# Bucketed attention with two expert layers: q and k read head columns first instead of being transposed on the chip

## The chip, the cores and the metric

The kernel runs on one core of one Trainium2 chip. The metric is the device time of one execution in microseconds (us), the median of several runs. The engines are TensorE (PE in the profile, PEld for its weight loads), VectorE (DVE), ScalarE (ACT), GpSimd (POOL) and SyncE (SP, which only issues transfers). Each works through its own instructions in the order in which they were written. The words q, k, v, s, p are the tiles of the attention, as below.

## The reference, cut to what matters

```python
def _attn_ref(q, k, v, proj):                    # q, k, v: (2, 8, 768, 64); proj: (64, 6)
    scale = 1.0 / np.sqrt(D)
    q_bits = (np.einsum('bhsd,dk->bhsk', q, proj) > 0).astype(np.int64)
    k_bits = (np.einsum('bhsd,dk->bhsk', k, proj) > 0).astype(np.int64)
    q_bucket = np.sum(q_bits * powers, axis=-1)
    k_bucket = np.sum(k_bits * powers, axis=-1)
    mask = q_bucket[:, :, :, None] == k_bucket[:, :, None, :]
    scores = scale * np.matmul(q, k.transpose(0, 1, 3, 2))
    scores = np.where(mask, scores, -1000000000.0)
    attn = np.exp(scores - np.max(scores, axis=-1, keepdims=True))
    attn = attn / (np.sum(attn, axis=-1, keepdims=True) + 1e-09)
    return np.matmul(attn, v)
...
x = attn_out.transpose(0, 2, 1, 3).reshape(B * S, H * D)
x = _moe_ref(x, ...)     # 8 experts, each token goes to one: relu(x @ w1[e]) @ w2[e], with two gates
return _moe2_ref(x, ...) # elu(x @ w_in) @ w_out
```

Sixteen heads of 768 tokens and 64 columns are attended; a query only sees the keys whose six projection signs equal its own. Then come a layer of eight experts and a dense layer.

## The kernel before

**Precision.** Matrix products run on operands split in two: hi is the value rounded by ScalarE to the fast format (fp32r), lo is the rest, computed by VectorE as value minus hi.

**Operands of a head.** The scores of a head come from four tiles of 128 rows by 768 columns, opnd[st, "qa"/"qb"/"ka"/"kb"], in four sets st = head % 4. Rows 0 to 63 of qa hold q hi, rows 64 to 127 q lo; ka holds k hi twice; rows 0 to 63 of qb hold q hi, of kb k lo. Rows 64 and up of qb and kb hold the signs of the projection (the bucket), scaled so that a pair of tokens in unlike buckets gets a large negative score. The first and the third 32 rows of that part are constants (constant_rows) or come from a tile z of signs.

**Tiles.** A tile n is 128 queries of one head; a head has 6, a pair of heads 12, the kernel 96 (8 pairs, counted 0 to 7). One turn of the loop at L951 does the following for several tiles at once, in this order: stage_M(n-1), the row maximum nm of the scores on VectorE (L367) and from it the scale sc and bias bi on GpSimd (L368, L369); what the list early holds; stage_T(n-3), six transpositions of the probabilities p on TensorE (L396) with hi on ScalarE (L398) and lo on VectorE (L399), in two halves; stage_S(n), four matmuls of scores into s (L349); stage_V(n-6), four matmuls with v (L413); stage_E(n-1), the exponential p on ScalarE (L376); now and then stage_O, the result o (L442), and stage_R, matmuls with the identity and the gate weights (L489). s has two buffers, so the scores of tile n wait for the exponential of tile n-2.

**Preparing a pair.** Beside the tiles of pair pr the operands of pair pr+1 are made, in six steps prep(pr+1, i), i = 0 to 5. Steps 0 to 3 are prep_T for q and k, in two halves of 384 tokens each: three TensorE transpositions of raw tokens (tokens on partitions, the columns of both heads side by side) into a PSUM tile prep (L212), hi from it on ScalarE (L217), lo on VectorE (L221 for q, L223 for k). When both halves of q or k stand, restack issues six transfers on SP that copy the rows of each head to their places in the operands (L300). Steps 4 and 5 are prep_Z: four matmuls with the projection (L278), and the sign compare on VectorE (L287); after the second, restack issues six small transfers of z. In pairs 1 to 6 the transposing steps are written after tiles 1, 2, 4 and 5 of the pair and finished in the next turn, so they lie in the six tiles that begin with the second; the steps of prep_Z come after tiles 7 and 8. In pair 0 the six steps come after tiles 3 to 8.

**Raw loads.** load_pair reads q and k of a pair as 128 partitions by 6 tokens by 64 columns, in runs of 64 values (L134), two transfers for q and two for k; v comes in one (L128).

**The opening.** Before the loop (L621 to L659) pair 0 is transposed the same way. Head 0's operands are copied into place by ScalarE and GpSimd (L635 to L640) and by three transfers (place, L656), head 1's by restack. The signs of the first keys come from first_Zk (two halves, three matmuls each) and those of the first queries from prep_Zm (six matmuls a half), both on hi and lo; first_Ze writes them straight into kb and qb of head 0 (L251). keep_warm runs matmuls on ones until the first data are there.

## Time and profile before

| what | us |
|---|---|
| median of three runs (lowest to highest) | 712.93 (712.04 to 713.87) |
| the profiled execution's own time | 713.77 |
| its span, from the first instruction to the last | 712.0 |
| attention tiles, first scores to last scores | 9.1 to 243.9 |
| TensorE busy in the span | 698.5 (98%) |
| VectorE / ScalarE busy in the span | 553.7 / 428.4 |

The profile is one execution. A group of rows gives, for one line and engine, a count and durations; the timeline gives single instructions with their start in us from the span's start and, in brackets, the idle time of the engine before one and what ended it. The stretches give, for a piece of the span, each engine's busy time and its number of instructions, then TensorE's granted clock (1.00 is 2.4 GHz), the share of the transfer engines and GB/s. Matmuls overlap, so TensorE's pace is read from the distance between starts.

### The profile page before, as it was taken

The page shows a single profiled execution, that of the slowest core. Times are in us where ns is not written, and L with a number is a line of the kernel's source. Part 1 is how long each engine was busy: PE and PEld are TensorE (multiplying, and loading weights), DVE is VectorE, ACT ScalarE, POOL GpSimd, SP SyncE. Part 2 cuts the span into 40 slices and gives each one's busy share as a digit, 9 for nine tenths or more (in the row PEclk, how much of TensorE's full clock was granted, in tenths as well). Part 3 has the DMA queues.
Part 4 walks back from the last instruction along what each step waited for, and adds up shares of the span by engine and source line. Part 5 has one row for each costly group of instructions (what it writes and reads, how often), then busy time and mean ns, then how long its engine had stood idle before and what let it go on. Part 6 is the DMA issues. An engine that isn't in the chain of part 4 may idle for free.

```text
span 712.0 us, 12226 instructions
## 1 busy us (share of the span) xinstructions
PE 698.5 (98%) x4211; PEld 626.8 (88%) x4212; DVE 553.7 (78%) x1046; ACT 428.4 (60%) x855; POOL 211.1 (30%) x508
## 2 busy tenths in 40 slices
PE   8999999999999999999999999999999999999996
PEld 6899999999998988999999998788888888888884
DVE  6989898899998997788888887877788547934433
ACT  6988888888888865666666665445443224422221
POOL 7665445455456661221065311000000000002012
PEclk9999999999999999999999999999999999999998
DMA  8857758686691239788878986322222000001011
GB/s 188 198 136 178 186 129 210 163 189 164 144 233 57 84 116 299 239 261 242 261 209 247 256 217 144 104 88 75 89 87 92 2 0 1 0 1 60 0 60 62
DMA packets 108596, 97.39 MB, mean 137 GB/s; under 512 B 33480, under 2 KB 94728, under 8 KB 108528
## 3 DMA queue, kind: packets, MB, share of 16 engines
q1 hardware_dynamic: 106064, 90.15, 47.3%
q0 software_dynamic: 2304, 6.40, 2.4%
q8 instruction: 35, 0.57, 0.3%
q14 instruction: 33, 0.27, 0.1%
q10 hardware_dynamic: 160, 0.00, 0.0%
HBM read 64.15 MB, written 10.72 MB: 105 GB/s over the span
## 4 chain that ended last, share of the span: by engine, by line
issue 32%; PE 23%; DMA 6%; POOL 1%; ACT 0%; SPq 0%; POOLq 0%; ACTq 0%
PE hps L1135 11%; PE yps L1148 7%; DMA out_dram<-part,tidt 5%; PE yps L1150 3%; DMA xs<-xs_d 1%; PE xTp L1117 1%; DMA tidt<-tid_d 1%; PE yps L1147 0%; POOL xs L857 0%; POOL out_dram L1293 0%; ACT sum L1153 0%; POOL spacer L612 0%; SPq L743 0%; POOLq L1293 0%; ACTq L1153 0%
## 5 line engine op out<-in xcount | busy, mean ns | idle before, releaser
L399 DVE TENSOR_TENSOR ptlo<-t,pthi 128x384 fp32r<-128x384 f32 x192 | 99.9, 548 | 14.7 <-ACT pthi L398 13.1
L376 ACT ACTIVATE p<-s,bi,sc 128x768 f32<-128x768 f32 x96 | 95.9, 999 | 17.5 <-POOL bi L369 15.7
L832 DVE TENSOR_TENSOR wl<-wraw,wh 128x1024 fp32r<-128x1024 f32 (+1 forms) x65 | 77.4, 1194 | 23.7 <-ACT wh L828 21.4
L367 DVE TENSOR_REDUCE nm<-s 128x1 f32<-128x768 f32 x96 | 90.9, 947 | 0.3 <-PE s L349 0.3
L398 ACT ACTIVATE pthi<-t 128x384 fp32r<-128x384 f32 x192 | 84.8, 497 | 10.2 <-PE t L396 8.9
L1293 POOL DMA_INDIRECT out_dram<-part,tidt x12 | 11.5, 960 | 263.5 <-DVE part L1290 262.2
L1255 ACT ACTIVATE ee<-gps 128x512 f32<-128x512 f32 x48 | 28.7, 597 | 98.0 <-PE gps L1245 98.0
L1148 PE MATMUL yps<-h,wh 128*128 128x448 f32 x256 | 84.4, 380 | 0.0
L396 PE MATMUL t<-ident,p 128*128 128x128 f32 x576 | 79.5, 273 | 0.0
L1245 PE MATMUL gps<-x2h,vl 128*128 128x512 f32 x192 | 75.9, 395 | 0.0
L1275 PE MATMUL a<-vh,gh 128*128 128x512 f32 x192 | 75.6, 394 | 0.0
L1275 PE MATMUL a<-vh,gl 128*128 128x512 f32 x192 | 75.4, 393 | 0.0
L1245 PE MATMUL gps<-x2h,vh 128*128 128x512 f32 x192 | 75.3, 392 | 0.0
L1245 PE MATMUL gps<-x2l,vh 128*128 128x512 f32 x192 | 75.2, 392 | 0.0
L1275 PE MATMUL a<-vl,gh 128*128 128x512 f32 x192 | 74.9, 390 | 0.0
L349 PE MATMUL s<-ka,qa 128*128 128x384 f32 x192 | 73.4, 383 | 1.2 <-DMA qa<-qlo 0.4
L1258 ACT ACTIVATE gh<-ee 128x512 fp32r<-128x512 f32 x48 | 30.4, 633 | 69.2 <-DVE ee L1257 69.2
L1256 DVE TENSOR_SCALAR ee<-ee 128x512 f32<-128x512 f32 x48 | 20.4, 426 | 66.3 <-ACT ee L1255 66.2
L396 PEld LDWEIGHTS t<-ident,p 128*128 128x128 f32 x576 | 67.4, 140 | 3.9 <-DVE ptlo L399 0.5
L828 ACT ACTIVATE wh<-wraw 128x1024 fp32r<-128x1024 f32 x63 | 66.2, 1052 | 2.7 <-DMA wraw<-in_moe_w_dram 2.7
L413 PE MATMUL o<-pthi,vst 128*128 128x384 f32 x192 | 66.9, 349 | 0.3
L349 PE MATMUL s<-kb,qb 102*128 102x384 f32 x192 | 65.3, 341 | 0.4 <-DMA kb<-z 0.4
(224 smaller groups left out, 1768.8 us busy)
## 6 DMA issues: line engine op xcount, KB each, us to landing
wraw<-in_moe_w_dram SPq DMA_DIRECT2D x64, 512.0 KB
w<-in_moe_w_in_dram SPq DMA_DIRECT2D x16, 512.0 KB
w<-in_moe_w_out_dram SPq DMA_DIRECT2D x16, 512.0 KB
ka<-khi SPq DMA_DIRECT2D x30, 192.0 KB
xs_d<-zt SPq DMA_DIRECT2D x8, 528.0 KB
xs<-xs_d SPq DMA_DIRECT2D x8, 528.0 KB
raw_v<-in_v_dram SPq DMA_DIRECT2D x8, 384.0 KB
kb<-klo SPq DMA_DIRECT2D x15, 192.0 KB
```

Source lines behind the costliest of these rows:

```text
L349: nc.tensor.matmul(ps[:, j, 0:HC], opnd[st, "q" + x][0:n1, cb], opnd[st, "k" + x][0:n1, j * HC:(j + 1) * HC], start=(x == "a"), stop=(x == ...
L367: nc.vector.tensor_reduce(nm, sps[n][:, :, 0:HC], AX.XY, ALU.max, negate=True)
L376: nc.scalar.activation(p.rearrange("p (a b) -> p a b", a=2), sps.pop(n)[:, :, 0:HC], AF.Exp, bias=bi, scale=sc, accum_out=sums[hd][:, c:c ...
L396: nc.tensor.transpose(ps[:, a, :], p[:, kt * 128:(kt + 1) * 128], ident)
L398: nc.scalar.activation(ho, ps, AF.Copy)
L399: nc.vector.tensor_tensor(lo[:, HALF * g:HALF * (g + 1), i * 128:(i + 1) * 128], ps, ho, ALU.subtract)
L413: nc.tensor.matmul(ops[m], vst[hd][:, kt, :], t[:, kt, :], start=(kt == 0 and x == 0), stop=(kt == NC - 1 and x == 1))
L832: fs = [lambda c=slice(j, j + h): eng.tensor_tensor(lo[:, c], r[:, c], hi[:, c], ALU.subtract) for j in range(0, PW, h)]
L1135: nc.tensor.matmul(ps, w[:, dc, fs], x[:, dc], start=(i == 0), stop=(i == len(terms) - 1))
L1148: nc.tensor.matmul(ps, wh[:, f], h[:, :, f], start=(f == 0), stop=last)
L1245: nc.tensor.matmul(ps, w[:, dc], x[:, dc, th * TC:(th + 1) * TC], start=(dc == 0 and i == 0), stop=(dc == KD - 1 and i == 2),)
L1275: nc.tensor.matmul(ps, x[:, cs], w, start=(fb in first_fb and i == 0), stop=(fb in last_fb and i == 2))
```

## The change

numpy now lays q and k out head by head with the 64 columns on partitions and the 768 tokens along them, each head twice: the array of one batch and pair has 256 rows, (head 0, head 0, head 1, head 1). The middle 128 rows are one head over the other, which is what prep_T had from its transpositions, so load_pair reads these in one transfer, in runs of 768 values, and prep_T takes hi and lo straight from the raw tile in SBUF. The six steps of pair 0 come one tile later (i = s - 4).

Heads 0 and 1 no longer go through prep_T and restack. load_twice reads each of them doubled (128 rows), and hi and lo are written in place by key_high, key_low, query_high, query_again and query_low: head 0 before the loop, the second half of its queries in turns 0 and 1, and head 1 partly before the loop (key_high) and partly after tiles 1 to 4 (the at(...) lines). The signs of head 0 come from the raw values with unsplit fp32 weights, one matmul a half (hash_of); those of head 1 from its finished operands (second_Z, four matmuls a half), compared by second_Ze and sent on by three transfers.

```diff
@@ load_pair, load_twice @@
-                t = ap2.tile([128, NC, 2 * D], F32, tag="raw_" + nm, name="raw_" + nm, bufs=2 if nm == "q" else 1)
...
-                        nc.sync.dma_start(
-                            t[:, c0:c0 + step, hh * D:(hh + 1) * D],
-                            src[b, h0 + hh].rearrange("(p c) d -> p c d", c=NC)[:, c0:c0 + step],
-                        )
+                t = ap2.tile([128, S], F32, tag="raw_" + nm, name="raw_" + nm, bufs=2 if nm == "q" else 1)
+                nc.sync.dma_start(t, src[b, h0 // 2, D:3 * D])
...
+    def load_twice(hd, nm, js, eng=nc.sync):
+        src = (q if nm == "q" else k)[0, 0, 2 * D * hd:2 * D * (hd + 1)]
...
+        cs = slice(js[0] * HC, (js[-1] + 1) * HC)
+        eng.dma_start(twice[hd, nm][:, cs], src[:, cs])
+
+    load_twice(0, "k", (0,))
+    load_twice(0, "q", (0,), nc.scalar)
+    load_twice(0, "k", (1,))
@@ prep_T @@
-        r = raw[pr, nm]
-        ps = prep_psum("prep")
-        for c in range(HALF):
-            cc = HALF * j + c
-            nc.tensor.transpose(ps[:, c * 128:(c + 1) * 128], r[:, cc, :], ident)
+        ps = raw[pr, nm][:, sl]
@@ heads 0 and 1 @@
+    def key_high(hd, j):
+        nc.scalar.activation(opnd[hd, "ka"][:, half(j)], twice[hd, "k"][:, half(j)], AF.Copy)
+
+    def key_low(hd, j, eng=nc.vector):
+        o, x, h = (t[0:64, half(j)] for t in (opnd[hd, "kb"], twice[hd, "k"], opnd[hd, "ka"]))
+        eng.tensor_tensor(o, x, h, ALU.subtract)
+
+    def query_high(hd, j):
+        nc.scalar.activation(opnd[hd, "qa"][:, half(j)], twice[hd, "q"][:, half(j)], AF.Copy, scale=SCALE)
...
+    def query_low(hd, j, c0=0, c1=HC):
+        cs = slice(j * HC + c0, j * HC + c1)
+        o, x = (t[64:128, cs] for t in (opnd[hd, "qa"], twice[hd, "q"]))
+        nc.vector.scalar_tensor_tensor(o, x, SCALE, o, ALU.mult, ALU.subtract)
+
+    def hash_of(ps, nm, j, i):
+        nc.tensor.matmul(ps, bdf[0:64, i], twice[0, nm][0:64, half(j)], start=True, stop=True)
...
+    def second_Z(j):
+        zps[1, j] = prep_psum("zps")
+        for i, (w, t, n) in enumerate(((0, "qa", 128), (2, "qa", 64), (1, "ka", 128), (1, "kb", 64))):
+            nc.tensor.matmul(
+                zps[1, j], bdr[0:n, w], opnd[1, t][0:n, half(j)], start=(i == 0), stop=(i == 3)
+            )
...
+        nc.vector.tensor_scalar(zt[0][0:64, half(j)], zps.pop((1, j))[0:64], 0.0, None, ALU.is_gt)
+        if j == 1:
+            restack(0, "z", (1,))
@@ the opening @@
+    load_twice(0, "q", (1,))
+    load_twice(1, "k", range(2))
+    load_twice(1, "q", range(2))
+    load_pair(0, "v")
+    load_pair(1)
+    keep_warm(8)
+    for j in range(2):
+        hash_of(zk[:, j, 0:HC], "k", j, 0)
+        key_high(0, j)
+    first_Zq(0)
+    query_high(0, 0)
+    query_again(0, 0, nc.scalar)
+    key_low(0, 0)
+    key_low(0, 1, nc.gpsimd)
...
+    query_high(0, 1)
+    for j in range(2):
+        key_high(1, j)
+    query_again(0, 1, nc.gpsimd)
@@ turns 1 to 4 @@
+    at(1, first_Zq, 1)
+    for i in range(2):
+        at(1 + i, query_high, 1, i)
+        at(2 + i, query_again, 1, i, nc.gpsimd)
+        at(2 + i, key_low, 1, i)
+        at(3 + i, query_low, 1, i)
+        at(3 + i, second_Z, i)
+        at(3 + i, lambda i=i: early.append(lambda: second_Ze(i)))
...
-            i = s - 3 if pr == 0 else s // 3 * 2 + s % 3 - 1 if s % 3 else -1
+            i = s - 4 if pr == 0 else s // 3 * 2 + s % 3 - 1 if s % 3 else -1
```

How this moves the instructions is shown at three places. A number behind a tile's name is only its buffer.

TensorE in the opening, up to the first scores of tile 0, before (zps takes the signs of the first queries, prep is a transposition, s the scores):

```order
L238 MATMUL zps<-qhi,bdh 128x384
L238 MATMUL zps<-qlo,bdh 128x384
L238 MATMUL zps<-qhi,bdl 128x384
L238 MATMUL zps<-khi,bdh 128x384
L238 MATMUL zps<-klo,bdh 128x384
L238 MATMUL zps<-khi,bdl 128x384
L212 MATMUL prep<-ident,raw_q 128x128 x3
L349 MATMUL s<-ka_130,qa_128 128x384 x2
```

The same place after, from the last warming matmul:

```order
L656 MATMUL warm<-ones_b 128x384
L263 MATMUL zk<-k_112,bdf 128x384 x2
L263 MATMUL zps<-q_114,bdf 128x384
L381 MATMUL s<-ka_124,qa_122 128x384 x2
L381 MATMUL s<-kb_125,qb_123 128x384 x2
```

Twelve transpositions and twelve sign matmuls ahead of the first scores (nine transpositions were ahead of the rows shown) have become three fp32 matmuls on the raw tiles.

VectorE in turns 1 to 4, from the maximum of tile 0 (nm), before; z is the sign compare of both heads:

```order
L367 TENSOR_REDUCE nm<-s 128x1
L221 SCALAR_TENSOR_TENSOR qlo<-prep,qhi 128x384
L367 TENSOR_REDUCE nm<-s 128x1
L251 TENSOR_SCALAR qb_129<-zps,thr,amp 38x384
L258 TENSOR_SCALAR z<-zps 128x384
L367 TENSOR_REDUCE nm<-s 128x1
L399 TENSOR_TENSOR ptlo<-t,pthi 128x3x128 x2
L258 TENSOR_SCALAR z<-zps 128x384
```

The same place after, from the maxima of tiles 0 and 1 (kb_129 and qa_126 belong to head 1):

```order
L399 TENSOR_REDUCE nm<-s 128x1 x2
L260 SCALAR_TENSOR_TENSOR qa_122<-q_114,qa_122 64x384
L274 TENSOR_SCALAR qb_123<-zps,thr,amp 38x384
L245 TENSOR_TENSOR kb_129<-k_172,ka_128 64x384
L399 TENSOR_REDUCE nm<-s 128x1
L431 TENSOR_TENSOR ptlo<-t,pthi 128x3x128 x2
L260 SCALAR_TENSOR_TENSOR qa_126<-q_174,qa_126 64x384
L245 TENSOR_TENSOR kb_129<-k_172,ka_128 64x384
L399 TENSOR_REDUCE nm<-s 128x1
L288 TENSOR_SCALAR z<-zps 64x384
```

Four low halves of head 1 now stand among the tiles (the fourth follows two lines on), and the compares z of head 1 come one tile later.

TensorE in pair 1, around the transposition of k for pair 2, before:

```order
L413 MATMUL o<-ptlo,vst 128x384
L212 MATMUL prep<-ident,raw_k 128x128 x3
L396 MATMUL t<-ident,p 128x128 x6
L349 MATMUL s<-ka_138,qa_136 128x384
L349 MATMUL s<-kb_139,qb_137 128x384
```

The same place after:

```order
L445 MATMUL o<-ptlo,vst 128x384
L428 MATMUL t<-ident,p 128x128 x6
L381 MATMUL s<-ka_132,qa_130 128x384
L381 MATMUL s<-kb_133,qb_131 128x384
L381 MATMUL s<-ka_132,qa_130 128x384
```

VectorE at that place before:

```order
L460 RECIPROCAL ri<-sm 128x3
L399 TENSOR_TENSOR ptlo<-t,pthi 128x3x128
L223 TENSOR_TENSOR klo<-prep,khi 128x384
L367 TENSOR_REDUCE nm<-s 128x1
L399 TENSOR_TENSOR ptlo<-t,pthi 128x3x128 x2
```

And after:

```order
L492 RECIPROCAL ri<-sm 128x3
L431 TENSOR_TENSOR ptlo<-t,pthi 128x3x128
L228 TENSOR_TENSOR klo<-raw_k,khi 128x384
L399 TENSOR_REDUCE nm<-s 128x1
L431 TENSOR_TENSOR ptlo<-t,pthi 128x3x128 x2
```

TensorE lost its three transpositions; VectorE does the same instructions in the same order, with the low part taken from two SBUF tiles instead of one of PSUM and one of SBUF.

## Rows read from the trace of the kernel before

**Rows 1.** The page, busy time by engine: us, share of the span, instructions.

```profile
PE 698.5 (98%) x4211; PEld 626.8 (88%) x4212; DVE 553.7 (78%) x1046; ACT 428.4 (60%) x855; POOL 211.1 (30%) x508
```

**Rows 2.** Stretches: start and end, length, then busy us of each engine.

```profile
16.98:24.13 7.15, 6.95 (x47) 5.49 (x45) 7.07 (x14) 6.90 (x16) 4.24 (x14) 1.00 0.72 180
...
68.81:83.10 14.29, 14.29 (x100) 13.60 (x97) 12.94 (x25) 13.22 (x31) 6.35 (x20) 1.00 0.67 185
83.10:98.60 15.50, 15.50 (x106) 15.25 (x105) 13.92 (x27) 12.92 (x29) 8.43 (x26) 1.00 0.82 190
...
188.52:203.11 14.59, 14.50 (x103) 13.71 (x103) 13.61 (x35) 13.46 (x32) 6.61 (x21) 1.00 0.75 195
```

**Rows 3.** Timeline, weight loads of TensorE in pair 2: start, us, what.

```profile
66.69 0.19 PEld L349 LDWEIGHTS s<-ka,qa 128*128 128x128 f32 x1
...
68.81 0.19 PEld L349 LDWEIGHTS s<-ka,qa 128*128 128x128 f32 x1
...
70.16 0.42 PEld L212 LDWEIGHTS prep<-ident,raw_q 128*128 128x128 f32 x3
71.21 0.19 PEld L349 LDWEIGHTS s<-ka,qa 128*128 128x128 f32 x1
...
75.95 0.19 PEld L349 LDWEIGHTS s<-ka,qa 128*128 128x128 f32 x1 [0.24 <-ACT p L376]
```

**Rows 4.** Instructions of single lines: count, shortest/median/longest ns, first and last start.

```profile
L212 PE MATMUL prep<-ident,raw_k x48: 270/272/421, 4.3 to 200.0; 128*128 128x128 f32 x48
...
L217 ACT ACTIVATE khi<-prep x16: 487/500/541, 5.2 to 201.4; 128x384 fp32r<-128x384 f32 x16
...
L223 DVE TENSOR_TENSOR klo<-prep,khi x16: 544/548/558, 5.7 to 202.2; 128x384 fp32r<-128x384 f32 x16
...
L423 POOL TENSOR_TENSOR osb<-o,o x26: 993/1011/1023, 39.3 to 222.4; 64x384 f32<-64x384 f32 x26
```

**Rows 5.** Timeline of the opening: start, us, engine, instruction, idle before.

```profile
4.11 0.31 ACT L187 ACTIVATE bdf<-pj 64x12 f32<-64x12 f32 x2 [0.35 <-DMA pj<-in_proj_dram]
...
6.19 0.52 PE L212 MATMUL prep<-ident,raw_q 128*128 128x128 f32 x3 [0.52 <-DMA raw_q<-in_q_dram]
...
7.86 1.29 DVE L251 TENSOR_SCALAR kb<-zk,thr,amp 38x384 fp32r<-38x384 f32 x2
...
9.18 0.86 DVE L251 TENSOR_SCALAR qb<-zps,thr,amp 38x128 fp32r<-38x128 f32 x2
...
10.35 0.96 DVE L367 TENSOR_REDUCE nm<-s 128x1 f32<-128x768 f32 x1 [0.31 <-PE s L349]
```

**Rows 6.** Timeline of TensorE: an unsplit fp32 matmul, three written, six recorded.

```profile
113.69 0.98 PE L489 MATMUL sp<-rw,osb 128*128 128x160 f32 x6
```

**Rows 7.** Timeline of pair 0: the sign rows z of the heads that follow.

```profile
15.96 0.55 DVE L258 TENSOR_SCALAR z<-zps 128x384 fp32r<-128x384 f32 x1
...
17.00 1.64 SPq L300 DMA_DIRECT2D kb<-z  x2
...
21.92 0.42 PE L349 MATMUL s<-kb,qb 102*128 102x384 f32 x1
...
34.15 0.74 SPq L300 DMA_DIRECT2D qb<-z  x1
...
36.94 0.42 PE L349 MATMUL s<-kb,qb 102*128 102x384 f32 x1 [0.38 <-DMA kb<-z]
```

**Rows 8.** Timeline: GpSimd beside VectorE instructions with one and with two SBUF inputs.

```profile
247.97 3.14 POOL L857 TENSOR_SCALAR xs<-xs 128x512 f32<-128x512 f32 x2
...
291.75 1.22 DVE L832 TENSOR_TENSOR wl<-wraw,wh 128x1024 fp32r<-128x1024 f32 x1 [0.49 <-ACT wh L828]
...
292.06 4.94 POOL L857 TENSOR_SCALAR xs<-xs 128x512 f32<-128x512 f32 x2 [13.01 <-DMA xs<-xs_d]
...
406.27 1.50 DVE L832 TENSOR_TENSOR wl<-wraw,wh 128x1024 fp32r<-128x1024 f32 x1 [0.38 <-ACT wh L828]
```

More of the change, by code (lines that the diff above doesn't have):

```diff
@@ L42 @@
     nc = tc.nc
-    B, H, S, D = q.shape
+    B, H, S, D = v.shape
     E, DM, F = w1.shape
@@ L166, in constant_rows @@
             nc.gpsimd.memset(opnd[st, nm][p0:p0 + n, c0:c1].bitcast(F32), a)
-    constant_rows(1, [(i, 0, S) for i in range(3)])
-    constant_rows(2, [(i, 0, S) for i in range(2)])
+    constant_rows(1, [(0, 0, S)])
     amp = ap1.tile([128, 1], F32, name="amp")
@@ L708 @@
             at(n, prep_V, p, i // 3, i % 3)
-    for n, st, i in ((1, 2, 2), (2, 3, 0), (6, 3, 1), (7, 3, 2)):
+    for n, st, i in ((4, 2, 0), (5, 2, 1), (6, 2, 2), (7, 3, 0), (8, 3, 1), (9, 3, 2)):
         for j in range(2):
@@ L1428 @@
     for name in _INS:
-        a = _np.ascontiguousarray(inputs[name])
+        a = inputs[name]
+        if name in ("q", "k"):
+            b, h, t, d = a.shape
+            a = a.reshape(b, h, 128, t // 128, d).transpose(0, 1, 4, 3, 2).reshape(b, h, 1, d, t)
+            a = _np.repeat(a, 2, axis=2).reshape(b, h // 2, 4 * d, t)
+        elif name == "proj":
+            a = _np.concatenate([a, a])
+        a = _np.ascontiguousarray(a)
         if a.dtype == _np.float64:
```

138 lines of the change are left out of this document (53 added, 85 removed).

## The prediction

> **What bounds the kernel now.** I read the page first: TensorE is busy 98% of the span, VectorE 78% [rows 1]. That would make every TensorE instruction worth its time, but a busy share is a mean over stages, so I went to the stretches. The change only touches the attention. In pair 2 the six tiles with transpositions of q and k take 14.29 us and the six that follow 15.50 [rows 2]. TensorE is full in both. The others are not alike: in the first six VectorE is busy 12.94 us and ScalarE 13.22, so 91% and 93%; in the next six 90% and 83%. The reader is to see that in the stretch that loses work, two more engines stand less than 10% behind TensorE.
>
> The timeline of weight loads gives the pace. A tile without preparation takes 2.12 us from its first scores to the next one's (66.69 to 68.81), one with a transposition 2.40 (68.81 to 71.21) [rows 3]. The transposition itself holds TensorE from its first load at 70.16; three loads spread over 0.42 us. And twice in the six tiles, first at 75.95, TensorE waits for the exponential p on ScalarE, there 0.24 us [rows 3]. So the pace there is already set in turns by TensorE and by the round through VectorE, GpSimd and ScalarE. The same six tiles stand in pairs 1 to 6; pair 6 has 14.59 us, with VectorE at 13.61 because the gate of the first half of the tokens runs beside it [rows 2].
>
> **Part 1, the six tiles of pairs 1 to 6.** Removed: four times three transpositions a pair. A single one is recorded with 0.27 us [rows 4], but they overlap, so their price is the tile's: 2.40 - 2.12 = 0.28 us, up to 0.35 by the spread of the loads; four make 1.1 to 1.4 us a pair. What TensorE keeps is six tiles of 2.12, so 12.7 us. Nothing leaves the others: hi stays one ScalarE instruction of 0.50 us and lo one VectorE instruction of 0.55 us [rows 4], now read from SBUF. The trace has a VectorE subtraction of two SBUF tiles, 1024 columns in 1.22 us [rows 8], 1.19 ns a column against 1.43 for the 384 columns from PSUM, the fixed part included; so I take the instruction itself at the same price. So ScalarE's 13.22 us [rows 2] becomes the longest share, and the question is how full it can get. In pair 0, from 16.98 to 24.13, VectorE is busy 7.07 of 7.15 us (99%) and ScalarE 6.90 (97%) [rows 2]: this loop can run with them nearly full. I take 98%: 13.22 / 0.98 = 13.5 us, 0.8 less than 14.29. For pair 6, 13.61 / 0.98 = 13.9, 0.7 less. Bounds: 12.7 us if the records' overlaps let ScalarE and VectorE keep up with TensorE (1.6 less), 14.1 if the round behind the two waits keeps its length (0.2 less). Six pairs: 5 x 0.8 + 0.7 = 4.7 us, from 1.2 to 9.6. The other six tiles of a pair have no transposition and stay at 15.5. A q or k load is one transfer instead of two and comes a pair ahead, so it is at nothing; its cover is the 30 us of a pair.
>
> **Part 2, the opening.** Now the maximum of tile 0 starts at 10.35 [rows 5]. Its data, both halves of k and one of q (576 KB), were in when TensorE's wait ended at 6.19; the first transposition at 4.3 [rows 4] had not waited for any. The changed kernel needs as many bytes, in longer runs; I take 5.0, bounds 4.3 and 6.2. The weights come from proj, awaited until 4.11 [rows 5], earlier than that. Then a sign matmul in fp32: three written ones of 160 columns are six records in 0.98 us, the last 0.30 long, so 0.136 each from start to start [rows 6], 0.27 for a written one and 384 / 160 x 0.27 = 0.65 us here. On VectorE there follow, after 5.65, the second compare of k (half of 1.29), the two compares of q (0.86) and the two pieces of query_low (0.28 and 0.42, by 0.55 for 384 columns): 2.2 us. The maximum of tile 0 starts at 7.9, 2.4 us earlier (1.2 to 3.1).
>
> **Part 3, given back in turns 1 to 6.** Both heads' low halves of k used to be made at once, before tile 0. Head 1's four low halves (two of k, two of q, 0.55 each) now stand among tiles 1 to 4, 2.2 us on a VectorE that is 99% busy [rows 2]. Behind them comes head 1's sign compare, and behind that three small transfers that tile 6, the first of head 1, waits for. Before the second compare of head 1 VectorE now has two more maxima (0.95 each), one more pair of low parts of p (about 1.0) and the four low halves. That is 5.1 us more than the 6.2 us that it takes now from the first maximum to the end of that compare (16.5 [rows 7]); 11.3 in all, less some 0.7 by overlap at their ends, puts its end at 7.9 + 10.6 = 18.5. SP then issues three transfers, the last 1.6 us after the first. In the trace the last of another such three is issued at 34.15, and its reader starts at 36.94 after a wait [rows 7]: 2.8 us. So 18.5 + 1.6 + 2.8 = 22.9 for tile 6, whose second score matmul now starts at 21.92 [rows 7]: 1.0 us later, in spite of the opening. Against that, two transpositions of k beside tiles 6 and 7 are gone (0.28 to 0.35 each), and TensorE's wait for the sign rows of head 2 ahead of 36.94 (0.4 us by that row) can shrink, though these come a turn later too. TensorE's wait at tile 6 also lets ScalarE and VectorE catch up. Together +0.2 us gained in pair 0; bounds -1.5 (both sign transfers awaited in full) and +2.4 (the whole of the opening is kept).
>
> **Sum.** 4.7 + 0.2 = 4.9 us. The profiled execution took 713.77, of which 712.0 is its span; it would take 708.9. The median of the runs shown, 712.93, lies 0.8 below that execution, so I predict 708.0 for the median. What ends the attention starts the expert layers, which are TensorE-bound and unchanged, so I let the gain through in full.
>
> **A price that may be missing: the port of GpSimd.** Two GpSimd multiplications took 3.14 us while VectorE ran instructions with one SBUF input, and 4.94 us beside L832, which has two; L832 itself took 1.50 instead of 1.22 at 406.27 [rows 8]. The low parts of q and k turn from the first sort into the second. The Trainium skill says so as a rule (SBUF — State Buffer, "SBUF: two separate sides"): a VectorE instruction with two SBUF inputs and a GpSimd instruction that reads SBUF exclude each other, and whichever starts first keeps the shared ports for the whole of its instruction. The trace agrees as to GpSimd's delay; of VectorE's it shows only 0.28 us, not a whole instruction. By the rule in full the time would come out slower, as in the third rival. In the sum I let VectorE's delay go into the 2% of slack.
>
> **Rivals.**
> First, TensorE stays the bound: six pairs of 1.6 and all of the opening, 9.6 + 2.4 = 12 us, 700.9. For it: in the 15.5 us stretch TensorE is dense with VectorE at 90%. Against: ScalarE's 13.22 us are more than TensorE's 12.7.
> Second, the round is the bound already: the two waits grow by what the transpositions free, 0.2 a pair, 1.2 + 0.2 = 1.4 us, 711.5. For it: these waits exist [rows 3]. Against: 97 to 99% in pair 0.
> Third, slower: in the six tiles each of the four low parts waits for the GpSimd instruction ahead of it, the sum of o (1.01 us [rows 4]) or a part of v (some 0.5), 0.75 us on average. On a VectorE that is the bound that is 3.0 a pair: 13.5 + 3.0 = 16.5 against 14.29, 2.2 x 6 = 13 us, 726. It decides from 0.8 / 4 = 0.2 us a low part on; the one delay in the rows is 0.28, but it is one of several meetings, and the low parts stand just before the maximum, when GpSimd is often done.
> That the change doesn't do what it says is out: the order shows no transposition of q or k left.
>
> **How the numbers follow.** Forecast, 706 to 710: 0.50. First rival 0.08, second 0.24, third 0.10, the remaining 0.08 between forecast and first rival. 0.3%, 2.1 us, is about what a measurement of this kernel can tell from no change, so faster means below 710.8 and slower above 715.1. Faster is the forecast, the first rival, what lies between, and 0.07 of the second: 0.73. Slower is the third: 0.10. Same: 0.17. The range from 703.5 to 712.0 takes in the second rival and leaves out the first and third.
>
> **What would show it.** In the changed profile the six tiles of pair 2 last 13.5 us (14.1 or more: second rival; 12.7: first), with ScalarE above 96% and TensorE waiting for p in most tiles. The first maximum starts at 7.9 and tile 6 at 22 to 23, its second score matmul behind a wait for a transfer of z. Low parts of q and k above 0.6 us, or GpSimd instructions beside them of twice their length, speak for the third rival. A 15.5 us stretch that changes, or expert layers whose length changes, would make the prediction wrong in a way I have no term for.

## The result, and the profile after

The changed kernel takes 721.33 us (median of 4 runs, 720.54 to 722.47), the kernel before in the same comparison 712.85 (4 runs, 712.04 to 713.87): 1.0118 times as long, 95% interval 1.0105 to 1.0131. It is slower by 8.5 us, where the forecast was 4.9 faster. The profiled execution has a span of 718.9 us against 712.0.

The page of the changed kernel, busy time by engine (compare [rows 1]):

```profile
PE 699.4 (97%) x4110; PEld 621.1 (86%) x4111; DVE 559.4 (78%) x1049; ACT 428.6 (60%) x855; POOL 215.5 (30%) x515
```

A hundred TensorE instructions are gone and TensorE is still busy 0.9 us longer. Where that comes from is seen by putting the starts of the row maximum nm of each tile beside each other, after minus before: tile 0 is 0.1 us early, tile 2 is 0.6 late, tile 3 1.8, tile 4 3.2, tile 5 5.2, tile 8 6.1; tile 12 is 9.0 late; then it shrinks, 8.6 at tile 24, 8.4 at tile 36, 7.75 at tile 95; the span ends 6.9 late. So there are four things to explain: the opening that gained nothing, 6 us lost in turns 2 to 5, 3 us lost at tile 12, and a gain of only about 0.2 us for each later pair.

**Turns 0 to 6.** Timeline of TensorE after (start, us, instruction, idle before):

```profile
3.88 3.09 PE L263 MATMUL zk<-k,bdf 64*128 64x384 f32 x4
6.76 1.48 PE L263 MATMUL zps<-q,bdf 64*128 64x384 f32 x2
8.55 1.01 PE L381 MATMUL s<-ka,qa 128*128 128x384 f32 x2 [0.31 <-DVE qa L260]
...
16.75 0.51 PE L381 MATMUL s<-kb,qb 102*128 102x384 f32 x1
17.85 0.79 PE L281 MATMUL zps<-qa,bdr 128*128 128x384 f32 x2 [0.59 <-DVE qa L260]
...
20.55 0.33 PE L381 MATMUL s<-kb,qb 102*128 102x384 f32 x1
22.15 0.78 PE L281 MATMUL zps<-qa,bdr 128*128 128x384 f32 x2 [1.27 <-DVE qa L260]
...
25.31 0.52 PE L381 MATMUL s<-ka,qa 128*128 128x384 f32 x1
...
28.37 0.41 PE L381 MATMUL s<-kb,qb 102*128 102x384 f32 x1 [0.74 <-POOL bi L401]
```

The same kind of score matmul is recorded with 0.51 and 0.52 us at 16.75 and 25.31 and with 0.33 at 20.55; before, those of turns 2 to 5 took 0.33 to 0.35 in a row and 0.41 to 0.44 behind another kind. Their starts are 0.32 us apart in the first case (384 columns at 1.2 GHz), 0.18 in the second (2.4 GHz). Until 17 us TensorE is at the low level: eight warm-up matmuls and three sign products (six records) stood back to back from 1.2 to 8.2 us without lifting it. It rises after 17, falls at 23.9, 1.8 us after the wait that ends at 22.15, and is back at 27.4. The stretches show the second fall in the granted clock (third number from the end; length, then busy us of PE, PEld, DVE, ACT, POOL):

```profile
18.00:22.00 4.00, 2.88 (x14) 1.82 (x14) 3.31 (x6) 1.84 (x4) 3.28 (x10) 1.00 0.00 0
22.00:26.00 4.00, 3.85 (x15) 3.04 (x16) 2.73 (x7) 1.58 (x4) 2.36 (x8) 0.74 0.02 4
26.00:30.00 4.00, 3.26 (x18) 2.97 (x17) 3.73 (x6) 3.25 (x7) 1.83 (x5) 0.83 0.21 44
```

The column shows only falls from the high level: it says 1.00 before 17 us, where the clock had never risen. The low start is read from the durations.

In the opening both sign compares of k (kb) on VectorE start only when the second product of k has ended, and the maximum of tile 0 (nm) waits for its scores. VectorE after, same columns:

```profile
7.00 1.29 DVE L274 TENSOR_SCALAR kb<-zk,thr,amp 38x384 fp32r<-38x384 f32 x2 [2.01 <-PE zk L263]
...
10.24 0.96 DVE L399 TENSOR_REDUCE nm<-s 128x1 f32<-128x768 f32 x1 [0.28 <-PE s L381]
```

The two waits of 0.59 and 1.27 us are a loop. VectorE and ScalarE after, same columns:

```profile
20.41 1.02 DVE L431 TENSOR_TENSOR ptlo<-t,pthi 128x384 fp32r<-128x384 f32 x2 [0.45 <-ACT pthi L430]
21.45 0.56 DVE L260 SCALAR_TENSOR_TENSOR qa<-q,qa 64x384 fp32r<-64x384 f32 x1
22.04 0.96 DVE L399 TENSOR_REDUCE nm<-s 128x1 f32<-128x768 f32 x1
...
24.27 0.49 ACT L430 ACTIVATE pthi<-t 128x384 fp32r<-128x384 f32 x1 [2.53 <-PE t L428]
```

Head 1's sign product (L281) stands on TensorE ahead of the next tile's transpositions of p (L428) and reads the low half of q (L260). That stands on VectorE behind the low parts of p (L431), which wait for the transpositions of the same turn. So each turn runs its engines one after the other.

At the end of the loop stands tile 6. Head 1's second sign compare on VectorE and the last transfer of its sign rows on SyncE:

```profile
23.71 0.55 DVE L288 TENSOR_SCALAR z<-zps 64x384 fp32r<-64x384 f32 x1 [0.72 <-PE zps L281]
...
25.97 0.74 SPq L332 DMA_DIRECT2D qb<-z  x1
```

The wait of 0.74 us ahead of tile 6's second score matmul at 28.37 is put down to bi, which that matmul doesn't read. It reads the sign rows, whose last transfer was issued 2.4 us earlier, so I take it for the wait on that transfer.

**Tile 12.** TensorE, VectorE and SyncE after:

```profile
38.39 0.55 DVE L319 TENSOR_TENSOR z<-zps,zb 64x384 fp32r<-64x384 f32 x1
...
40.38 0.93 SPq L131 DMA_DIRECT2D raw_k<-in_k_dram  x1
41.41 1.64 SPq L332 DMA_DIRECT2D kb<-z  x2
...
42.56 0.45 PE L381 MATMUL s<-ka,qa 128*128 128x384 f32 x1
45.92 0.41 PE L381 MATMUL s<-kb,qb 102*128 102x384 f32 x1 [2.91 <-DMA kb<-z]
```

Before, tile 12 waited 0.38 us for its sign rows [rows 7], and their last transfer was issued 2.8 us ahead of the reader. Now pair 1 is prepared one turn later (s - 4 for s - 3). The signs stand at 38.94, SyncE issues them at 41.41, behind k's rows and the next load, and TensorE waits 2.91 us.

**The six tiles of pair 2.** The stretches that answer to 68.81:83.10 and 83.10:98.60 in [rows 2]:

```profile
77.47:91.49 14.02, 13.49 (x87) 12.35 (x85) 13.28 (x25) 13.30 (x31) 6.68 (x20) 1.00 0.61 155
91.49:106.99 15.50, 15.50 (x105) 15.26 (x105) 13.81 (x27) 12.92 (x29) 8.42 (x26) 1.00 0.70 195
```

14.02 us for 14.29: 0.27 gained, not 0.8. TensorE lost 1.1 us of work there (four times the 0.28 of the prediction), and most of that went into its waits for the exponential. The waits of its weight loads (us in total, times, longest), before in 68.8 to 83.15:

```profile
PEld s L349 <- ACT p L376: 0.5, 2, 0.2
```

After, in 77.4 to 91.5:

```profile
PEld s L381 <- ACT p L408: 1.2, 3, 0.5
```

VectorE has 0.34 us more to do than before, with the same instructions. The low parts, by form, in 76.84 to 91.02 (count, busy us, mean ns):

```profile
L226 DVE SCALAR_TENSOR_TENSOR qlo<-raw_q,qhi 128x384 fp32r<-128x384 f32 x2 | 1.3, 648 | 0.0
L228 DVE TENSOR_TENSOR klo<-raw_k,khi 128x384 fp32r<-128x384 f32 x2 | 1.3, 628 | 0.0
```

They took 548 ns before [rows 4]. One of each two is long, and GpSimd's sum of the two output halves (L455) was already running when it started. Where the low part started first, it kept its length and GpSimd's instruction, a part of v (L360, 0.46 us otherwise), was long:

```profile
80.34 1.01 POOL L455 TENSOR_TENSOR osb<-o,o 64x384 f32<-64x384 f32 x1
81.02 0.75 DVE L226 SCALAR_TENSOR_TENSOR qlo<-raw_q,qhi 128x384 fp32r<-128x384 f32 x1
...
90.56 0.55 DVE L228 TENSOR_TENSOR klo<-raw_k,khi 128x384 fp32r<-128x384 f32 x1
90.63 0.79 POOL L360 TENSOR_TENSOR vst<-raw_v,vst 128x128 fp32r<-128x128 f32 x1
```

Of the 28 low parts 12 take 0.71 to 0.86 us (ten beside L455, two beside L360), the others 0.54 to 0.58; before, all 32 had 0.54 to 0.56, beside L423 (the same sum) too, when they read PSUM.

### The profile page after: what moved, and what is told of

Its sections match the earlier page's. It is cut to its first block, busy times and chain, and to the rows that moved or that the text cites. A ratio compares the mean times of both kernels' runs of the same rounds, so it can differ in the third digit from the quotient of the medians.

```text
span 718.9 us, 12007 instructions
## 1 busy us (share of the span) xinstructions
PE 699.4 (97%) x4110; PEld 621.1 (86%) x4111; DVE 559.4 (78%) x1049; ACT 428.6 (60%) x855; POOL 215.5 (30%) x515
## 4 chain that ended last, share of the span: by engine, by line
PE 38%; issue 34%; DVE 10%; ACT 8%; DMA 7%; POOL 3%; DVEq 0%; POOLq 0%; SPq 0%; ACTq 0%
PE hps L1157 9%; PE yps L1170 7%; PE s L381 5%; DMA out_dram<-part,tidt 5%; ACT p L408 4%; PE o L445 4%; PE t L428 4%; PE yps L1172 3%; DVE ptlo L431 3%; DVE nm L399 3%; ACT pthi L430 2%; PE sp L521 2%; PE zps L310 1%; PE xTp L1139 1%; DVE qlo L226 1%
## 5 line engine op out<-in xcount | busy, mean ns | idle before, releaser
L431 DVE TENSOR_TENSOR ptlo<-t,pthi 128x384 fp32r<-128x384 f32 x192 | 100.0, 547 | 13.0 <-ACT pthi L430 12.0
L428 PE MATMUL t<-ident,p 128*128 128x128 f32 x576 | 80.6, 277 | 0.0
L381 PE MATMUL s<-ka,qa 128*128 128x384 f32 x192 | 76.0, 397 | 4.3 <-ACT p L408 3.5
L428 PEld LDWEIGHTS t<-ident,p 128*128 128x128 f32 x576 | 69.6, 142 | 4.2 <-issue 0.4
L381 PE MATMUL s<-kb,qb 102*128 102x384 f32 x192 | 66.9, 350 | 3.6 <-DMA kb<-z 2.9
```

Source lines behind the costliest of these rows:

```text
L381: nc.tensor.matmul(ps[:, j, 0:HC], opnd[st, "q" + x][0:n1, cb], opnd[st, "k" + x][0:n1, j * HC:(j + 1) * HC], start=(x == "a"), stop=(x == ...
L428: nc.tensor.transpose(ps[:, a, :], p[:, kt * 128:(kt + 1) * 128], ident)
L431: nc.vector.tensor_tensor(lo[:, HALF * g:HALF * (g + 1), i * 128:(i + 1) * 128], ps, ho, ALU.subtract)
```

## The experiments

All comparisons are against the kernel before, measured on the same chip beside each run. Intervals are for the ratio. "Tile n late by" means the start of nm of tile n, this kernel's profile minus that of before. In e3_preps and e4_all the fill of head 3's constant rows comes behind the transfer of its sign rows and overwrites a part of them; all other kernels compute the whole.

### One cause at a time

**e1_warm**: more warm-up.

```diff
-    keep_warm(8)
+    keep_warm(13)
```

> The changed kernel with 13 instead of 8 warm-up matmuls ahead of the first sign matmul; nothing else. Theory A (TensorE stays at 1.2 GHz until 17 us because its opening no longer lifts the clock): the first score matmuls start 0.18 us apart instead of 0.32, the six score matmuls and sign products of turns 0 to 3 lose about 3 us together, and the kernel takes about 718 us instead of 721.3. Theory B (the loss of pair 0 is the order: VectorE's low half of head 1 stands behind the low parts of the same turn, and TensorE waits for it with the second head's sign product): the waits of 0.6 and 1.3 us ahead of that product stay, whatever the clock, and no more than 1 us is gained, 720.5.

Measured 725.64 us, 1.016 (1.013 to 1.019), some 4 us slower than the change. The first thirteen matmuls ran back to back from 1.2 to 5.4 us and the clock still did not rise; the sign products only came 1.5 us later. TensorE in e1:

```profile
2.73 2.77 PE L656 MATMUL warm<-ones_b 128*128 128x384 bf16 x8
5.43 2.93 PE L263 MATMUL zk<-k,bdf 64*128 64x384 f32 x4
...
15.58 0.52 PE L381 MATMUL s<-kb,qb 102*128 102x384 f32 x1
```

So five more warm-ups are not the lever. A is not tested by this, since the clock stayed low.

**e2_head1**: head 1's steps one turn earlier.

```diff
-        at(1 + i, query_high, 1, i)
-        at(2 + i, query_again, 1, i, nc.gpsimd)
-        at(2 + i, key_low, 1, i)
-        at(3 + i, query_low, 1, i)
+        at(i, query_high, 1, i)
+        at(1 + i, query_again, 1, i, nc.gpsimd)
+        at(1 + i, key_low, 1, i)
+        at(2 + i, query_low, 1, i)
```

> The changed kernel with the four vector-side steps of head 1 (high half, its copy, key's and query's low half) one turn earlier, so that the query's low half no longer stands in the turn of the sign product that reads it. Theory B: TensorE's two waits ahead of the second head's sign product (0.6 and 1.3 us) go, ScalarE's two waits of 2.4 and 2.5 us for the transposed tile shrink to under 1, and with the waits the fall of the granted clock at 24 us; 717.5 us. Theory A: until 17 us nothing moves, at most 1.9 us are gained, and the score matmuls of 9 to 17 us still start 0.32 us apart.

Measured 721.65 us, 1.0117 (1.0100 to 1.0134): no gain. Both waits went, as B said, and TensorE was without a gap from 12 to 24 us; but the clock, up at 4.4 us this time, fell at 7.9 and stayed low until 21.5, so that until then the score matmuls started 0.32 us apart, as A said; a turn took 4.9 us, and tile 6 then waited 1.43 us for its sign rows. B's 4 us did not come. Taking the waits away moved the time to the clock and the transfer.

**e3_preps, e3b_preps**: pair 1 prepared from turn 3 again; in e3b also its constant rows one turn earlier.

```diff
-    for n, st, i in ((4, 2, 0), (5, 2, 1), (6, 2, 2), (7, 3, 0), (8, 3, 1), (9, 3, 2)):
+    for n, st, i in ((3, 2, 0), (4, 2, 1), (5, 2, 2), (6, 3, 0), (7, 3, 1), (8, 3, 2)):
...
-            i = s - 4 if pr == 0 else s // 3 * 2 + s % 3 - 1 if s % 3 else -1
+            i = s - 3 if pr == 0 else s // 3 * 2 + s % 3 - 1 if s % 3 else -1
```

> The changed kernel with pair 1's preparation started in turn 3 of pair 0 instead of turn 4, as the kernel before had it. Theory C (tile 12 waits 2.9 us because the sign rows of pair 1 stand one turn later in the transfer queue): the wait at tile 12 falls under 0.5 us, and 2.5 us are gained to the end, 718.8. Rival D (the queue is simply full there, whatever the order): the wait moves to the rows of q and k of tile 6 to 12 or stays over 2 us, and the time stays within 1 us of 721.3.

> The changed kernel with pair 1's preparation from turn 3, and the constant rows of pair 1 also one turn earlier, so that none of them waits for a transfer of sign rows. Theory C: tile 12's wait of 2.9 us falls under 0.5, tile 24 is 6 us behind the kernel before instead of 8.65, 718.8 us. Rival D: the wait turns up at tiles 6 to 11, since pair 1's transfers now stand ahead of or beside those of tile 6, and the time stays above 720.

e3 took 726.03 us: GpSimd's fill waited for the transfer that it came to stand behind, and with it the scale and bias of the next tile. GpSimd in e3:

```profile
44.12 0.77 POOL L172 MEMSET kb<- 32x384 f32 x2 [6.48 <-DMA kb<-z]
```

e3b took 718.77 us, 1.0079 (1.0063 to 1.0096). Tile 12's wait is gone (its second score matmul follows the first by 0.36 us) and 2.6 us of the 8.5 with it: C holds.

**e4_all**: e1, e2 and e3 together.

> The three edits together: 13 warm-up matmuls, head 1's steps one turn earlier, pair 1's preparation from turn 3. If A, B and C each hold for their part and add, tile 24 starts as late after the span's start as in the kernel before or up to 1 us earlier (the changed kernel: 8.65 us later), and the kernel takes 711.5 to 713.5 us, that is, no better than before, since the six-tile stretches of pairs 1 to 6 gave back only about 0.2 us each. If only one cause is real, it stays above 716.

Measured 723.46 us, 1.0140 (1.0123 to 1.0158), with e3's wait and e1's late opening in it. It tells nothing of its own.

### TensorE's clock and its share

**e5_rows**: head 0's sign products over 128 rows. **e6_pe**: with it, four warm-ups behind the query's product, and head 1's products in the order 128, 128, 64, 64 rows.

```diff
-        nc.tensor.matmul(ps, bdf[0:64, i], twice[0, nm][0:64, half(j)], start=True, stop=True)
+        nc.tensor.matmul(ps, bdf[:, i], twice[0, nm][:, half(j)], start=True, stop=True)
```

And in e6 alone:

```diff
     first_Zq(0)
+    keep_warm(4)
...
-        for i, (w, t, n) in enumerate(((0, "qa", 128), (2, "qa", 64), (1, "ka", 128), (1, "kb", 64))):
+        for i, (w, t, n) in enumerate(((0, "qa", 128), (1, "ka", 128), (2, "qa", 64), (1, "kb", 64))):
```

> The changed kernel with the fp32 sign products of head 0 reading all 128 rows of the doubled data instead of 64 (twice the sum, the same signs); nothing else. Theory A1 (the low clock follows from the 64-row fp32 products, which stand where the kernel before had products over 128 rows): the clock rises before the first score matmul in spite of only 8 warm-up matmuls, score matmuls 0.18 us apart from the first on, tile 0's maximum at 9.0 instead of 10.24, tile 4 less than 2.5 us behind the kernel before instead of 3.2; 718 to 719.5 us. Rival A2 (the clock falls because of TensorE's gap of 0.3 to 1 us ahead of the first scores and the waits of turns 3 and 4, whatever the rows): 0.32 us apart until at least 12 us, no gain, 721.

> As the 128-row kernel, with four warm-up matmuls more behind the query's first sign product, so that TensorE has work up to the first scores, and with the second head's four sign products in the order 128, 128, 64, 64 rows instead of 128, 64, 128, 64. If the clock is what costs pair 0 its 5 us (theory A): all score matmuls of pair 0 are 0.18 us apart from 8.5 us on, the four products take 1.1 instead of 1.48 us, and 3 to 4 us are gained, 717.5. If the in-order waits on VectorE are the larger part (theory B): the two waits of 0.6 and 1.3 us stay or grow, the clock falls again at 20 to 28 us, and 720 us is not undershot.

e5's clock rose at 5.9 us with the same eight warm-ups, and its tile 3 was late by 0.1 us instead of 1.8. Yet it took 722.71 us, 1.0134 (1.0117 to 1.0151): no gain. TensorE in e5:

```profile
9.91 0.34 PE L381 MATMUL s<-kb,qb 102*128 102x384 f32 x1
...
16.18 0.78 PE L281 MATMUL zps<-qa,bdr 128*128 128x384 f32 x2 [1.56 <-DVE qa L260]
...
20.47 0.78 PE L281 MATMUL zps<-qa,bdr 128*128 128x384 f32 x2 [1.26 <-DVE qa L260]
...
26.69 0.66 PE L381 MATMUL s<-kb,qb 102*128 102x384 f32 x1 [1.43 <-DMA qb<-z]
27.15 0.53 PE L381 MATMUL s<-ka,qa 128*128 128x384 f32 x1
...
45.33 0.41 PE L381 MATMUL s<-kb,qb 102*128 102x384 f32 x1 [2.71 <-DMA kb<-z]
...
48.00 0.52 PE L381 MATMUL s<-kb,qb 102*128 102x384 f32 x1
```

What the opening won was lost again, 3.2 us of it between tiles 3 and 5 with the clock up, where TensorE now waited longer for VectorE's low half than in the change. Then came the waits for sign rows at tiles 6 and 12; the clock fell during the first and 1.6 us after the second (low from 26.4 to 29.8 and from 46.9 to 50.3 us). e6 took 719.36 us, 1.0096 (1.0076 to 1.0116): 2 us less than the change; tile 8 was late by 3.2 us, TensorE's two waits for VectorE (1.57 and 1.37 us) and tile 12's (2.83) stayed, as theory B had it.

### The repairs together

**e7_all**: e6, head 1's whole chain one turn earlier still (products in turns 2 and 3), e3b. **e8_pool**: with it, GpSimd's fills of pair 0 spread and six warm-ups in turn 1. **e12_const**: with that, head 2's constant rows copied by ScalarE in the opening.

```diff
-        at(1 + i, query_high, 1, i)
-        at(2 + i, query_again, 1, i, nc.gpsimd)
-        at(2 + i, key_low, 1, i)
-        at(3 + i, query_low, 1, i)
-        at(3 + i, second_Z, i)
+        if i:
+            at(0, query_high, 1, i)
+        at(i, query_again, 1, i, nc.gpsimd)
+        at(i, key_low, 1, i)
+        at(1 + i, query_low, 1, i)
+        at(2 + i, second_Z, i)
```

e8 against e7, with some other fills and bit-weight steps of GpSimd moved by a turn or more:

```diff
     query_again(0, 1, nc.gpsimd)
+    constant_rows(1, [(1, 0, S), (2, 0, S)])
...
     at(1, first_Zq, 1)
+    at(1, keep_warm, 6)
```

e12 against e8:

```diff
+    for nm, p0, n in (("qb", 64, 32), ("qb", 96, NBITS), ("kb", 64, 32)):
+        nc.scalar.activation(opnd[2, nm][p0:p0 + n], opnd[1, nm][p0:p0 + n], AF.Copy)
```

> All repairs together: 128-row sign products, the four warm-up matmuls, the products' order, head 1's whole chain one turn earlier still (sign products in turns 2 and 3, its low parts a turn ahead of them), pair 1's preparation from turn 3 with the constant rows of pair 1 one turn earlier. If pair 0's loss is the low clock, the waits for VectorE, and the late sign rows of tiles 6 and 12 and nothing else, tile 24 comes within 1 us of the kernel before (the changed kernel: 8.65 us later), and the six-tile stretches give 0.2 us per pair as in the changed kernel: 711 to 713.5 us. If a cause is missing, it stays above 715.

> As the kernel with all repairs, and GpSimd's work of pair 0 spread (constant rows of head 1 in the opening, one block of pair 1's in turn 2, the last two bit-weight steps and one fill later), with six warm-up matmuls in turn 1, where TensorE was idle for 2.3 us. Theory G (what is left of pair 0's loss, 2.5 us at tile 8, is GpSimd: the scale and bias of tiles 2 to 5 stand behind its fills and copies, and exp waits 0.7 to 0.9 us for them): exp's waits for the bias in tiles 3 to 5 fall under 0.4 us, tile 8 is within 1 us of the kernel before, and the kernel takes 713.5 to 714.5 us. If not, the time stays at 715.8.

> As the kernel with GpSimd's work spread, and the three blocks of constant rows of head 2 copied by ScalarE in the opening, where it waits 3 us, instead of filled by GpSimd in turns 2, 4 and 5 (0.77 us each). Theory G (the scale and bias of tiles 4 to 6 stand behind GpSimd's fills): exp's waits of 0.36 and 0.81 us in turns 5 and 6 go, tile 8 is 0.7 us behind the kernel before instead of 1.7, 712.4 us. If the waits stay because of the bit weights and the values' casts, 713.4.

e7 took 715.76 us, 1.0039 (1.0025 to 1.0053); e8 713.36, 1.0004 (0.9995 to 1.0012), no different from before; e12 714.20, 1.0019 (1.0010 to 1.0028). e7 missed its forecast, so a cause was missing. With all repairs 8 of 8.5 us came back, though e1, e2 and e5 alone brought nothing and e3b 2.6. So the loss lies in what these edits touch together: the low clock, the loop through VectorE, the late sign rows and GpSimd's queue; how it divides among them isn't shown. e8 alone makes two edits, and the medians of e7 and e8 lie 2.4 us apart, their profiled executions only 0.9 (714.01 and 713.07), 0.8 of it at tile 8, where exp's longest waits for its bias in turns 3 to 6 went from 0.81 and 0.87 to 0.36 and 0.81 us. Four of the five runs of e7 have a granted clock of 0.992 to 0.995, the profiled one 0.997, so a part of the 2.4 may be the clock and not GpSimd. In e8 tile 8 is still late by 1.7 us, and e12 (1.7) shows that head 2's constant rows are not why. That rest is unexplained.

### What the pairs are bound by

**e10_dummy**: e8 with twelve transpositions a pair put back, into a tile nobody reads.

```diff
+        idle = prep_psum("idle")
+        for c in range(HALF):
+            nc.tensor.transpose(idle[:, c * 128:(c + 1) * 128], ps[:, c * 128:(c + 1) * 128], ident)
```

> As the kernel with GpSimd's work spread, and the twelve transpositions per pair put back on TensorE for pairs 1 to 7, into a PSUM tile that nobody reads (the result comes from the same data as without them). Theory R (TensorE's time there was cover): pairs 2 to 6 take 0.2 to 0.3 us more each, 1.5 to 2 us in all. Theory T (TensorE sets the six tiles, as the forecast had it): 12 times 0.11 us more per pair, 1.3 us, 8 to 9 us in all.

Measured 715.58 us, 1.0035 (1.0022 to 1.0049). The same stretch of pair 2 (e8 14.02 us from first scores to first scores) takes 14.43, a pair 0.2 to 0.45 us more: R. Put back, 1.3 us of TensorE a pair cost 2.2 us in all.

**e9_hi**: e8 with the high parts of pairs 1 to 7 on GpSimd. **e11_hilo**: with it, k's low parts too. **e13_hi_early, e14_khi_early**: e12 with the high parts of pairs 2 to 7 (e14: k's alone) on GpSimd one turn ahead of the low parts.

```diff
         def evac_hi():
-            nc.scalar.activation(hi[:, sl], ps, AF.Copy, scale=sc if nm == "q" else 1.0)
+            if nm == "q":
+                nc.gpsimd.tensor_scalar(hi[:, sl], ps, sc, None, ALU.mult)
+            else:
+                nc.gpsimd.tensor_copy(hi[:, sl], ps)
```

> As the kernel with GpSimd's work spread, and the high parts of q and k of pairs 1 to 7 written by GpSimd instead of ScalarE. Theory R (the turns with preparation are set by the round through VectorE and ScalarE, both 95% busy there, not by TensorE): ScalarE loses 2 us per pair, VectorE's 95% then sets the stretch, and each pair from 1 to 6 is 0.3 to 0.6 us shorter, 2 to 4 us in all. Rival P (GpSimd's copies beside VectorE's low parts lengthen these, 0.55 to 0.75 us as the 81.02 us row of the changed kernel): low parts at 0.7 us or more, no gain.

> As the kernel with the high parts on GpSimd, and also k's two low parts per pair on GpSimd instead of VectorE (1.0 us each there, 0.55 on VectorE). Theory R: VectorE loses another 1.1 us per pair, and the pairs from 1 to 6 get 0.2 to 0.5 us shorter again. Rival Q (GpSimd's queue becomes the round: scale and bias stand behind 1.5 us of preparation): exp waits for the bias longer, and the pairs get longer than with the high parts alone.

> As the kernel with head 2's constant rows on ScalarE, and for pairs 2 to 7 the high parts written by GpSimd one turn ahead of the low parts, so that VectorE does not wait for them. Theory R1 (ScalarE sets the turns with preparation): each of these four turns loses 0.2 to 0.4 us, 1 us per pair, 707 us. Theory R2 (VectorE sets them, or the chain maximum, bias, exp, transposed high and low part): 0 to 0.3 us per pair, 711 to 712.4. Rival Q (GpSimd's 1.2 us for q's high part delays scale and bias): the pairs get longer by 0.3 us or more, 714 or worse.

> As the kernel before it in this list, but with only k's two high parts (0.5 us each) on GpSimd one turn ahead, q's on ScalarE as in the changed kernel. R1: the fifth and sixth tile of each stretch lose 0.2 to 0.4 us each, 0.6 us per pair, 709 us; R2: no more than 0.2 per pair, 711.5 to 712.4; Q cannot be seen here, since GpSimd is idle 1.4 us in these turns.

e9 took 739.67 us, 1.0369 (1.0352 to 1.0386). GpSimd needs 1.20 us for q's high part, and VectorE, in order, stood waiting with everything behind it:

```profile
80.91 1.20 POOL L223 TENSOR_SCALAR qhi<-raw_q 128x384 fp32r<-128x384 f32 x1
...
82.14 0.56 DVE L229 SCALAR_TENSOR_TENSOR qlo<-raw_q,qhi 128x384 fp32r<-128x384 f32 x1 [1.43 <-POOL qhi L223]
```

Neither R nor P: the wait that the edit itself made decided (16.0 us in all for q's high parts, 12.5 for k's). e11 (733.50 us, 1.0283, 1.0265 to 1.0301) is better than e9 because k's low parts then stand behind the high parts on the same engine, and VectorE no longer waits for those. e13 took 720.26 us, 1.0094 (1.0078 to 1.0110), e14 715.42, 1.0037 (1.0023 to 1.0050). Without the wait the tile with k's second high part got 0.09 us shorter (2.37 for 2.46 from maximum to maximum, mean of pairs 2 to 6), the one before it 0.36 longer, since scale and bias stood behind GpSimd's copy: R2 and Q. ScalarE's share alone does not set these turns.

**e15_add**: e8 with GpSimd's sum of the output halves two turns later for the first 22 half heads. **e16_later**: e8 with the low parts of pairs 2 to 7 one turn later instead.

```diff
-            add.append((3 * m + (11 if m else 13), t, w[r0:r0 + 64], u[r0:r0 + 64]))
+            add.append((3 * m + (13 if m < 22 else 11), t, w[r0:r0 + 64], u[r0:r0 + 64]))
```

> As the kernel with GpSimd's work spread (713.4 us), and GpSimd's addition of the two output halves (1.0 us) two turns later for the first 22 half heads, so that it no longer runs beside the low parts of q and k. Theory S (a low part that reads SBUF on VectorE is slowed by GpSimd's two-input additions): the low parts of pairs 2 to 7 that took 0.71 to 0.86 us take 0.55, the second and fifth tile's turns lose 0.2 us each, pairs 2 to 5 take 29.2 instead of 29.5 to 30.0, and 1.5 to 2 us are gained: 711.5. Rival: VectorE's time there is cover as well, or the addition delays scale and bias in the turn it is moved to: the low parts get shorter and the pairs do not, 713 to 714.

> As the kernel with GpSimd's work spread (713.4 us), and for pairs 2 to 7 each low part of q and k one turn later than its high part, so that the first of each two no longer stands beside GpSimd's addition but in the short third turn. Theory S with VectorE as the bound (R2): the low parts take 0.55 us, the second and fifth tile's turns lose 0.5 us or more each, the third turns (1.84) grow by 0.46, and a pair loses 0.2 to 0.4 us net: 711 to 712. If the turns are set by the chain and not by VectorE's load: the third turns grow by 0.46 us and the others lose less, 714 to 716.

e15 took 737.34 us, 1.0331 (1.0310 to 1.0351). S holds for the low parts: q's are 0.55 us, with a single 0.72, and the second tile's turn is 2.69 us for 2.90. But the sums then came too late for the products of the attention's output (L521), and TensorE waited 13.7 us for them; the rest of the 24 us was not followed up. The low parts of q in e8 (count, shortest/median/longest ns):

```profile
L226 DVE SCALAR_TENSOR_TENSOR qlo<-raw_q,qhi x14: 541/564/894, 19.3 to 194.9; 128x384 fp32r<-128x384 f32 x14
```

The same in e15:

```profile
L226 DVE SCALAR_TENSOR_TENSOR qlo<-raw_q,qhi x14: 547/550/722, 19.8 to 215.2; 128x384 fp32r<-128x384 f32 x14
```

TensorE's waits for the sums in e15, 30 to 260 us (us in total, times, longest):

```profile
PE sp L521 <- POOL osb L455: 13.7, 10, 1.5
```

e16 took 715.43 us, 1.0030 (1.0013 to 1.0048): all but two of its 28 low parts are 0.54 or 0.55, the second tile's turn fell from 2.90 to 2.27 (maximum to maximum, mean of pairs 2 to 6), but the third rose from 2.32 to 2.89 and the fourth from 1.85 to 2.36; the six together went from 14.50 to 14.91. From first scores to first scores the six got 0.1 shorter (14.37 to 14.26), but the tile behind them, into which the last low part now falls, took 3.88 us for 3.59 in pair 2. Relieving one engine of these turns moved the length, it did not take it away.

## Why the prediction was wrong, point by point

**Part 1, the six tiles: mechanism wrong, and the second rival right.** The step that failed is 13.22 / 0.98: that ScalarE would fill to 98% once TensorE had room. It filled to 95% (13.30 of 14.02), as did VectorE (13.28), and TensorE waits for p in three tiles of six instead of two. I had read TensorE's 14.29 of 14.29 busy us [rows 2] as its bound, while the 0.24 us wait at 75.95 [rows 3] was the better sign: the stretch hung on the round through VectorE, GpSimd and ScalarE, and TensorE's transpositions were cover. The term was 4.7 us; the nm starts show 1.2 (9.0 to 7.75 from tile 12 to 95), which is what the second rival gave, and e10 shows it from the other side. That VectorE and ScalarE reach 97 to 99% in pair 0 [rows 2] did not mean that they reach it with another mix of instructions.

**The port.** I let it go into slack. The rows now show it: 12 low parts 0.16 to 0.31 us longer, 2.7 us of VectorE in all. That reaches the point of 0.2 us from which the third rival was to decide, but in fewer than half of the low parts, and its 3.0 us a pair didn't come. The Trainium skill (SBUF — State Buffer, "SBUF: two separate sides") has the one that starts first, a VectorE instruction with two SBUF inputs or a GpSimd instruction that reads SBUF, keep the shared ports for its whole instruction. In these meetings the trace agrees: in 13 low parts that started beside a running L455 or L360 the end came 0.41 or 0.42 us after GpSimd's, so of their 0.55 us only 0.13 passed while GpSimd ran; seven L360 that started beside a running low part took 0.75 to 0.81 instead of 0.46 us; and there was no delay when the low part had one operand in PSUM. What I mis-sized was the time left of the sum: I had 0.75 us on average, and the low parts start 0.17 to 0.44 us before its end. On the path little of it arrived: e10, with TensorE's old work and the new low parts, loses 0.5 us to the kernel before from tile 12 to 84, six pairs, where e8 gains 1.5.

**Part 2, the opening: a term of 2.4 us that was 0.1.** Two steps failed. The first is 0.65 us for a sign product. A sign product is two records, and the two products of k, four records at 1.2 GHz, take 3.09 us. I had priced them from [rows 6], in a stage at 2.4 GHz, and never asked at which level TensorE would be after a shorter warm-up. So VectorE's compares of k start at 7.00 where I had 5.65; 0.3 us of that is the data, in at 5.3 and not at 5.0. The second is that I put one compare of k (0.65 us) and no score matmul behind the product: both compares stand there, 1.29 us, and nm waits 0.28 for its scores. Together that is 2.3 us, the distance from 7.9 to 10.24. With the clock up (e6) nm starts at 8.84, 1.5 us earlier than before, still 0.9 after my 7.9; e8 has 9.67, where a low part of head 1 stands ahead of it on VectorE.

**Part 3, pair 0: +0.2 became -6 at tile 8.** I priced VectorE's 2.2 us and the transfers, in engine time. The step that failed is that head 1's product and low halves were added up as if they could overlap with the turn: on three in-order engines they form a ring (rows above), which stretched the time from tile 3's maximum to tile 4's to 3.8 us and from there to tile 5's to 4.3, with the clock falling in it. Tile 6 I had at 22.9; its second score matmul starts at 28.37. Of these 5.5 us the late opening is 2.3. From the first maximum to the end of head 1's second compare I had 10.6 us and it took 14.0 (10.24 to 24.26), 3.4 more. The way from there through the transfers I had right: 4.4 us, measured 4.1.

**Tile 12, not in the sum.** The prediction names that its sign rows "come a turn later too" and lets the wait shrink. It grew from 0.38 to 2.91 us. The failed step is the queue: SyncE has k's transfers and the next load ahead of them.

**Outside the sum.** The expert layers got 1 us shorter: from their first product into yps to the first into gps 163.9 us, before 164.9. All kernels with the new layout have 163.1 to 164.2. Before, TensorE waits there 0.21 and 1.22 us for GpSimd's xs (L857), after 0.31 once, which is the 1 us; in the same place ScalarE waits 2.4 us for a load of weights before and not after. No run tests why.

**What stays open**: the 1.7 us of pair 0 left in e8, and which chain of the round sets the prepared turns; ScalarE's and VectorE's load each alone do not. No version here beats the kernel before.

## What to carry to other kernels

A busy share of 100% on an in-order engine with pipelined records is not proof that it is the bound: look for the first wait inside the stretch and ask which round it belongs to, or put the work back into an unread tile, as e10 did. When a step is moved into a pipeline written out turn by turn, follow it as a ring: who waits in order for it, and what that engine still has to deliver to the engine that makes it. And price TensorE work at the start of a kernel at the level of the clock that the rows there will have, not at the one of the steady state.
